# Longer rows for K and V in a cached attention block: 16 KB loads, P transposed on VectorE, PV in four row tiles

## The chip, the cores and the metric

The kernel runs on one core of a Trainium2 chip. The metric is the device time of one execution in microseconds. The time before is the median of three runs.

## The reference

A block of grouped-query attention reads a cache: 32 batches, 4 new tokens each, 32 query heads, 4 heads of K and V, 2048 cached tokens of 128 elements, all in bf16.

```python
q = (x @ wq).reshape(B, Sq, Hq, Dh).transpose(0, 2, 1, 3)      # B 32, Sq 4, Hq 32, Dh 128
k = jnp.repeat(k_cache, rep, axis=1)                           # k_cache: [32, 4, 2048, 128]
v = jnp.repeat(v_cache, rep, axis=1)
scores = jnp.einsum("bhqd,bhkd->bhqk", q, k) * (Dh ** -0.5)
p = softmax(scores, axis=-1)
o = jnp.einsum("bhqk,bhkd->bhqd", p, v)
return o.transpose(0, 2, 1, 3).reshape(B, Sq, Hq * Dh) @ wo    # D 1024
```

One batch needs 2 MB of K and 2 MB of V. For each head of K and V there are 32 rows of queries (8 heads of 4 tokens), so the scores of a batch are 128 rows (4 heads by 32) by 2048 tokens.

## The kernel before

A small `Program` class holds a list of operations for each engine, in the order in which that engine runs them, with the events that each waits for. The order is written out by hand, and no planner moves anything.

**Loads.** SP issues everything: x, then a `stream` of 2 MB loads that go round 9 slots: four of wq, K of batches 0 to 2, then V of a batch and K of the batch three further on, in turn, and at the end four of wo (the last one in four parts). A load waits until the load that had its slot before is used up (`freed`). K and V of one batch are laid out as "g (p t) d -> p g (t d)" with p = 128: each partition gets 16 consecutive tokens of each of the four heads, which is four rows of 4 KB. A row of wq is 16 KB, a row of wo 2 KB.

**Start.** x is transposed, the Q projection runs over eight banks of PSUM, and K of the first two batches is transposed.

**One batch i on TensorE:** `qk(i)`, then `pv(i-1)`, then the transposes of K of batch i+2 (`kt_fill`, eight fills of eight 128x128 tiles), then the transposes of P of batch i (`tr_fill`, four fills of four tiles).

- `qk` makes 16 matmuls in four column tiles of 32, one tile for each head, 512 tokens each, into the four banks of `ps_s`.
- The fills go round a ring of four banks of PSUM, a, b, c and o. VectorE copies some of them to SBUF and ScalarE the others (`consumer`): of K's eight fills five go to VectorE, of P's four two.
- P is transposed by matmuls against a diagonal matrix, `diag`, that holds the reciprocal of each row's sum, so that P is normalized in the same step.
- `pv` makes 64 matmuls of a full 128x128 array with 32 columns each, 16 accumulating over the tokens for each of the four heads, into bank o.

**VectorE** takes the maximum of each row over the 2048 scores (line 379), scales it (380), copies the output of the batch before into `oT_sb` (368), makes reciprocal and `diag` (388, 389), and copies its share of the fills (353). **ScalarE** makes exp with the row's sum (408) and copies its share (355). The next `qk` waits for exp of the batch before, as the scores have one set of banks.

**End.** After the last `pv` the output projection, 64 matmuls of 512 columns over the four loads of wo (line 318), two copies, and the store.

Of the kernel before, what the change touches and what calls it, by code (L numbers as in the profile page):

```python
# [6 lines left out]
ALU = mybir.AluOpType  # L7
# [47 lines left out]
def bass_standalone__gqa_block_cached__sampling_kernel(  # L55
# [17 lines left out]
    G = Hkv  # L73
    scale = float(Dh) ** -0.5
    NSLOT = 9
    SLOT = 8192
    NRING = 4
    KT_FILLS = 2 * G
    TR_FILLS = 4
    AHEAD = 2  # L80
    WQ_LOADS = 4
    WO_LOADS = 4
    HPL = Hq // WO_LOADS

# [5 lines left out]
    with ExitStack() as es:  # L90
        sb = lambda name, shape, dt: es.enter_context(nc.sbuf_tensor(name, shape, dt))
        slots = sb("slots", [128, NSLOT, SLOT], BF16)
        KT_sb = sb("KT_sb", [128, 2, G, Sk], BF16)
        QT_sb = sb("QT_sb", [128, B, Hq, Sq], BF16)
        oT_sb = sb("oT_sb", [128, Hq, NT], BF16)
        pp_sb = sb("pp_sb", [128, 2, Sk], BF16)
        ident = sb("ident", [128, 128], BF16)
        diag = sb("diag", [128, 2, 128], BF16)
# [4 lines left out]
        P_sb = pp_sb[:, 0, :]  # L103
        PT_sb = pp_sb[:, 1, :].rearrange("p (t r) -> p t r", r=128)
        x_sb = pp_sb[:, 0, 0:D]
        xT_sb = pp_sb[:, 0, D:2 * D].rearrange("p (a b) -> p a b", b=128)
        out_sb = pp_sb[:, 1, 0:D]

        ps_s = es.enter_context(nc.psum_tensor("ps_s", [128, Sk], F32))
        ring = [es.enter_context(nc.psum_tensor(f"ps_{c}", [128, 512], F32)) for c in "abco"]  # L110
        ring_f32 = [p[:, :] for p in ring]
        ring_bf16 = [p.bitcast(BF16) for p in ring_f32]
        ps_o = ring_f32[3]
# [3 lines left out]
        for n in ["x", "out"] + [f"slot{i}" for i in range(NSLOT)] + [f"wo{i}" for i in range(4)]:  # L117
            pr.sems[n] = es.enter_context(nc.semaphore(f"s_{n}"))
# [3 lines left out]
        for b in range(AHEAD + 1):  # L122
            stream.append(("k", b))
        for b in range(B):
            stream.append(("v", b))
            if b + AHEAD + 1 < B:
                stream.append(("k", b + AHEAD + 1))
# [13 lines left out]
        pr.load("sp", lambda e: e.dma_start(x_sb, x_flat[:, :]), "x", "x", 16)  # L141
        for n, l in enumerate(stream):
            kind, i = l
            waits = [freed(stream[n - NSLOT])] if n >= NSLOT else []
            s, v = f"slot{n % NSLOT}", 16 * (n // NSLOT + 1)
            if kind == "wq":
                fn = lambda e, l=l, i=i: e.dma_start(slot(l), wq_v[:, i, :])  # L147
            elif kind in "kv":
                src = (k_cache if kind == "k" else v_cache)[i].rearrange("g (p t) d -> p g (t d)", p=128)
                fn = lambda e, l=l, src=src: e.dma_start(slot(l).rearrange("p (g f) -> p g f", g=G), src)  # L150
            if kind != "wo":
                pr.load("sp", fn, l, s, v, waits)
                continue
            last = i == WO_LOADS - 1
            parts = 4 if last else 1
            per = HPL // parts
            for q in range(parts):
                fn = lambda e, l=l, i=i, q=q, per=per: e.dma_start(
                    slot(l)[:, q * per * D:(q + 1) * per * D].rearrange("p (h n) -> p h n", n=D),
                    wo_v[:, i * HPL + q * per:i * HPL + (q + 1) * per, :],  # L160
                )
                if last:
                    pr.load("sp", fn, ("wo", i, q), f"wo{q}", 16, waits)
                else:
                    pr.load("sp", fn, l, s, v, waits)
# [4 lines left out]
        jobs = [("kt", b, f) for b in range(AHEAD) for f in range(KT_FILLS)]  # L170
        for i in range(B):
            if i + AHEAD < B:
                jobs += [("kt", i + AHEAD, f) for f in range(KT_FILLS)]
            jobs += [("tr", i, f) for f in range(TR_FILLS)]
        job_index = {j: n for n, j in enumerate(jobs)}

        def consumer(job):
            kind, _, f = job
            if kind == "kt":
                return "act" if f in (4, 6, 7) else "dve"  # L180
            return "dve" if f in (0, 2) else "act"

        def ring_waits(job):
            n = job_index[job]
            if n < NRING:
                return [("q_evac", n)]
            w = [("evac",) + jobs[n - NRING]]
            if n % NRING == 3:
                b = job[1] - AHEAD - 1 if job[0] == "kt" else job[1] - 1
                if b >= 0:  # L190
                    w.append(("ot", b))
            return w


        pr.op("pool", lambda e: e.memset(ident[:], 0.0), [], "zero")
        pr.op("pool", lambda e: e.affine_select(
            out=ident[:], in_=ident[:], compare_op=ALU.not_equal, fill=1.0, base=0,
            pattern=[[-1, 128]], channel_multiplier=1), ["zero"], "ident")
# [33 lines left out]
        def kt_fill(b, f):  # L232
            job = ("kt", b, f)
            dst = ring_bf16[job_index[job] % NRING]
            g, half = f // 2, f % 2

            def fn(e):
                for q in range(8):
                    t = half * 8 + q
                    ins = e.transpose(  # L240
                        dst[:, q * 128:(q + 1) * 128],
                        slot(("k", b))[:, (g * NKT + t) * Dh:(g * NKT + t + 1) * Dh],
                        ident[:, :],
                    )
                return ins

            pr.op("pe", fn, [("k", b)] + ring_waits(job), job)

        def tr_fill(b, f):
            job = ("tr", b, f)  # L250
            dst = ring_f32[job_index[job] % NRING]

            def fn(e):
                for q in range(4):
                    t = f * 4 + q
                    ins = e.matmul(dst[:, q * 128:(q + 1) * 128], lhsT=P_sb[:, t * 128:(t + 1) * 128],  # L256
                                   rhs=diag[:, b % 2, :], start=True, stop=True)
                return ins

            pr.op("pe", fn, [("exp", b), ("diag", b)] + ring_waits(job), job)  # L260

        def pv(b):
            def fn(e):
                v = slot(("v", b))
                for g in range(G):
                    for t in range(NKT):
                        ins = e.matmul(  # L267
                            ps_o[:, 32 * g:32 * (g + 1)],
                            lhsT=v[:, (g * NKT + t) * Dh:(g * NKT + t + 1) * Dh],
                            rhs=PT_sb[:, t, 32 * g:32 * (g + 1)],  # L270
                            start=(t == 0),
                            stop=(t == NKT - 1),
                        )
                return ins

            w = [("v", b)] + [("evac", "tr", b, f) for f in range(TR_FILLS)]
            if b > 0:
                w.append(("ot", b - 1))
            pr.op("pe", fn, w, ("pv", b))

        def qk(i):
            def fn(e):
                for c in range(Sk // 512):
                    for g in range(G):
# [3 lines left out]
                            rhs=KT_sb[:, i % 2, g, c * 512:(c + 1) * 512],  # L288
# [4 lines left out]
                return ins  # L293

            w = [("evac", "kt", i, f) for f in range(KT_FILLS)]
# [175 lines left out]
```

## Time and profile before

| | |
|---|---|
| median of three runs | 389.67 us (389.29 to 390.6) |
| profiled execution | 388.88 us |
| its span, first to last instruction | 386.9 us |
| mean granted TensorE clock | 0.938 of full speed |
| read from HBM | 151.26 MB, 392 GB/s over the span |
| busy: TensorE, VectorE, ScalarE | 296.0, 242.4, 196.6 us |

The profile is of one execution. A page gives busy times, the span in 40 slices (tenths of busy time, granted clock, GB/s), the DMA queues, the chain of work that ended last, and the costliest groups of instructions. In a group's row stand line, engine, operation, output and inputs, shapes and count, then busy time and mean duration in ns of one, then the idle time before them and what ended it. In a row of the timeline stand start and duration in microseconds, engine, line and operation. "PEld" is TensorE's loading of weights. In a row of the stretches stand the stretch, its length, each engine's busy time (with its count of instructions), the granted clock, the share of the DMA engines and GB/s.

### The profile page before, as it was taken

How to read it: one execution, taken by the hardware profiler on the slowest of the kernel's cores; microseconds unless marked ns; L12 is line 12 of the kernel's file. 1: busy time of each engine (PE TensorE's matmuls, PEld its weight loads, DVE VectorE, ACT ScalarE, POOL GpSimd, SP SyncE). 2: the span in 40 equal slices, each digit the busy share in tenths (PEclk: the TensorE clock that was granted, in tenths of full speed). 3: DMA queues.
4: the chain of work that ended last, by engine and by line, in shares of the span. 5: the costliest groups of instructions: out<-in, count | busy, mean ns of one | idle time of the engine just before them, and what ended most of it. 6: DMA issues, size and time to landing. Idle time of an engine off the chain costs nothing.

```text
span 386.9 us, 11667 instructions
## 1 busy us (share of the span) xinstructions
PE 296.0 (77%) x5448; PEld 246.8 (64%) x5448; DVE 242.4 (63%) x390; ACT 196.6 (51%) x230; POOL 0.7 (0%) x6
## 2 busy tenths in 40 slices
PE   2877787776977977878788869877777787886596
PEld 1777576665766766767667657666666677664542
DVE  0026787775777777758777757877777577774400
ACT  1024766652655565466564635666555564664300
POOL 0000000000000000000000000000000000000000
PEclk9999999998999899889898979999999898997689
DMA  8999999999999999999999999999999999999981
GB/s 327 430 412 410 407 404 407 408 408 409 406 406 409 407 409 410 406 409 407 407 409 409 405 410 410 405 409 408 407 407 407 408 409 407 409 408 359 372 327 56
DMA packets 38912, 152.26 MB, mean 393 GB/s; under 512 B 1232, under 2 KB 1232, under 8 KB 38352
## 3 DMA queue, kind: packets, MB, share of 16 engines
q1 hardware_dynamic: 38864, 151.52, 98.5%
q8 instruction: 42, 0.69, 0.7%
q14 instruction: 6, 0.05, 0.0%
HBM read 151.26 MB, written 0.26 MB: 392 GB/s over the span
## 4 chain that ended last, share of the span: by engine, by line
DMA 87%; PE 7%; ACT 2%; DVE 2%; SPq 1%; issue 0%
DMA slots<-in_k_cache_dram 87%; PE ps_s L318 4%; DVE mx L379 1%; ACT pp_sb L408 1%; PE ps_s L285 1%; ACT KT_sb L355 1%; PE ps_a L240 1%; PE ps_o L267 0%; SPq L147 0%; PE ps_o L256 0%; PE ps_a L256 0%; PE ps_b L240 0%; SPq L150 0%; PE ps_c L256 0%; PE ps_b L256 0%
## 5 line engine op out<-in xcount | busy, mean ns | idle before, releaser
L408 ACT ACTIVATE pp_sb<-ps_s,negmx 128x2048 bf16<-128x2048 f32 x32 | 62.9, 1967 | 93.1 <-DVE negmx L380 93.1
L379 DVE TENSOR_REDUCE mx<-ps_s 128x1 f32<-128x2048 f32 x32 | 73.3, 2292 | 35.3 <-PE ps_s L285 35.3
L240 PE MATMUL ps_a<-ident,slots 128*128 128x128 bf16 x512 | 43.8, 234 | 42.2 <-DMA slots<-in_k_cache_dram 41.3
L240 PEld LDWEIGHTS ps_a<-ident,slots 128*128 128x128 bf16 x512 | 33.7, 105 | 46.1 <-DMA slots<-in_k_cache_dram 44.9
L267 PEld LDWEIGHTS ps_o<-pp_sb,slots 128*128 128x128 bf16 x2048 | 53.5, 96 | 14.6 <-issue 13.7
L267 PE MATMUL ps_o<-pp_sb,slots 128*128 128x32 bf16 x2048 | 56.7, 177 | 0.8 <-ACT pp_sb L355 0.8
L355 ACT ACTIVATE KT_sb<-ps_a 128x1024 bf16<-128x1024 bf16 x32 | 32.6, 1020 | 45.6 <-PE ps_a L240 45.6
L240 PE MATMUL ps_o<-ident,slots 128*128 128x128 bf16 x512 | 42.7, 231 | 7.8 <-DVE KT_sb L353 7.8
L353 DVE COPY KT_sb<-ps_b 128x1024 bf16<-128x1024 bf16 x64 | 43.7, 683 | 5.2 <-PE ps_b L240 5.2
L353 DVE COPY KT_sb<-ps_a 128x1024 bf16<-128x1024 bf16 x32 | 22.1, 689 | 35.0 <-PE ps_a L240 35.0
L240 PE MATMUL ps_c<-ident,slots 128*128 128x128 bf16 x512 | 43.3, 233 | 0.7 <-issue 0.7
L240 PE MATMUL ps_b<-ident,slots 128*128 128x128 bf16 x512 | 43.5, 234 | 0.0
L240 PEld LDWEIGHTS ps_o<-ident,slots 128*128 128x128 bf16 x512 | 33.8, 105 | 11.4 <-DVE KT_sb L353 11.2
L240 PEld LDWEIGHTS ps_c<-ident,slots 128*128 128x128 bf16 x512 | 34.8, 105 | 1.5 <-issue 0.9
L240 PEld LDWEIGHTS ps_b<-ident,slots 128*128 128x128 bf16 x512 | 35.2, 106 | 0.4
L285 PE MATMUL ps_s<-KT_sb,QT_sb 128*32 128x512 bf16 x512 | 34.3, 389 | 0.0
L355 ACT ACTIVATE KT_sb<-ps_c 128x1024 bf16<-128x1024 bf16 x32 | 32.7, 1021 | 1.9 <-PE ps_c L240 1.9
L355 ACT ACTIVATE KT_sb<-ps_o 128x1024 bf16<-128x1024 bf16 x32 | 32.9, 1027 | 0.0
L353 DVE CAST pp_sb<-ps_a 128x512 bf16<-128x512 f32 x32 | 22.1, 692 | 12.8 <-PE ps_a L256 12.8
L256 PE MATMUL ps_o<-diag,pp_sb 128*128 128x128 bf16 x128 | 13.2, 227 | 14.7 <-ACT KT_sb L355 14.7
L353 DVE CAST pp_sb<-ps_c 128x512 bf16<-128x512 f32 x32 | 21.9, 685 | 1.9 <-PE ps_c L256 1.6
L353 DVE COPY KT_sb<-ps_c 128x1024 bf16<-128x1024 bf16 x32 | 21.9, 684 | 1.0 <-PE ps_c L240 1.0
(46 smaller groups left out, 244.7 us busy)
## 6 DMA issues: line engine op xcount, KB each, us to landing
slots<-in_k_cache_dram SPq DMA_DIRECT2D x32, 2048.0 KB, 25.0
slots<-in_v_cache_dram SPq DMA_DIRECT2D x32, 2048.0 KB, 24.2
slots<-in_wq_dram SPq DMA_DIRECT2D x4, 2048.0 KB, 14.9
slots<-in_wo_dram SPq DMA_DIRECT2D x3, 2048.0 KB, 25.6
slots<-in_wo_dram SPq DMA_DIRECT2D x4, 512.0 KB, 12.2
pp_sb<-in_x_dram SPq DMA_DIRECT2D x1, 256.0 KB, 2.7
out_dram<-pp_sb SPq DMA_DIRECT2D x1, 256.0 KB, 2.2
```

Of the source, the lines that this page charges most:

```text
L240: ins = e.transpose(dst[:, q * 128:(q + 1) * 128], slot(("k", b))[:, (g * NKT + t) * Dh:(g * NKT + t + 1) * Dh], ident[:, :],)
L256: ins = e.matmul(dst[:, q * 128:(q + 1) * 128], lhsT=P_sb[:, t * 128:(t + 1) * 128], rhs=diag[:, b % 2, :], start=True, stop=True)
L267: ins = e.matmul(ps_o[:, 32 * g:32 * (g + 1)], lhsT=v[:, (g * NKT + t) * Dh:(g * NKT + t + 1) * Dh], rhs=PT_sb[:, t, 32 * g:32 * (g + 1)], ...
L285: ins = e.matmul(ps_s[32 * g:32 * (g + 1), c * 512:(c + 1) * 512], lhsT=QT_sb[:, i, REP * g:REP * (g + 1), :], rhs=KT_sb[:, i % 2, g, c * ...
L318: ins = e.matmul(ps_s[:, c * 512:(c + 1) * 512], lhsT=oT_sb[:, h, :], rhs=w[:, h - i * HPL, c * 512:(c + 1) * 512], start=(h == 0), stop=( ...
L353: pr.op("dve", lambda e: e.tensor_copy(dst, src), w, ("evac",) + job)
L355: pr.op("act", lambda e: e.activation(dst, src, ACT.Copy), w, ("evac",) + job)
L379: pr.op("dve", lambda e, i=i: e.tensor_reduce(mx[:, i:i + 1], ps_s[:, :], AX.X, ALU.max), [("qk", i)], ("max", i))
L408: pr.op("act", lambda e, i=i: e.activation(P_sb, ps_s[:, :], ACT.Exp, bias=negmx[:, i:i + 1], scale=scale, accum_out=ssum[:, i:i + 1]), [( ...
```

## The change

- K and V are laid out as "g (p t) d -> (g p) (t d)" with p = 32: each head has 32 partitions, and each partition 64 consecutive tokens, one row of 16 KB.
- A transpose of K now gives 32 tokens of each of the four heads; `KT_sb` is [d, 64 steps, 4 heads, 32 tokens], and `qk` reads it in runs of 32. `qk` is split in four, each with the wait for its own two fills. VectorE copies fills 0 to 3, ScalarE 4 to 7.
- P is transposed on VectorE in 32x32 blocks, SBUF to SBUF, with one instruction for a batch. `tr_fill` and `diag` go.
- `pv` makes 256 matmuls: 64 steps by four row tiles, one row tile for each head, with 32 tokens of V as the stationary operand and 32 columns. Each head has a bank of the ring to itself. One more matmul writes the reciprocals as a row on all partitions (`R_bank`).
- ScalarE copies that row and the four heads' raw output to SBUF (`raw_evac`), ahead of exp of batch i; VectorE multiplies the two into `oT_sb` (`ot_scale`). The fills of K that follow a `pv` in the ring wait for `raw_evac`, and a `pv` waits for the copies of the last four fills.
- `pv` runs two batches behind `qk` (LAG 2) in place of one; K is loaded four batches ahead of V in place of three; there are 8 slots in place of 9.
- wo is loaded by POOL in 16 parts, each of which waits for V of batch 30 to land, besides its slot.

The core of the diff:

```diff
-    NSLOT = 9
+    NSLOT = 8
+    LAG = 2
+    LEAD = AHEAD + LAG
...
-                src = (k_cache if kind == "k" else v_cache)[i].rearrange("g (p t) d -> p g (t d)", p=128)
+                src = k_cache[i].rearrange("g (p t) d -> (g p) (t d)", p=KP)
+                src = v_cache[i].rearrange("g (p t) d -> (g p) (t d)", p=KP)
...
+                for q in range(WO_PARTS):
+                    part = slot(l)[:, q * WO_PER * D:(q + 1) * WO_PER * D].rearrange("p (h n) -> p h n", n=D)
+                    h0 = i * HPL + q * WO_PER
+                    pr.load("pool", fetch(part, wo_v[:, h0:h0 + WO_PER, :]), ("wo", i, q), f"wo{i * WO_PARTS + q}", 16, waits + [("v", B - 2)])
...
         def pv(b):
+            waits = list(bank_last.values())
+            for n in range(NRING):
+                bank_last[n] = ("raw", b)
             def fn(e):
-                v = slot(("v", b))
-                for g in range(G):
-                    for t in range(NKT):
+                v = slot(("v", b)).rearrange("p (t d) -> p t d", d=Dh)
+                for t in range(KTOK):
+                    for g in range(G):
+                        rows = slice(KP * g, KP * (g + 1))
                         ins = e.matmul(
-                            ps_o[:, 32 * g:32 * (g + 1)],
-                            lhsT=v[:, (g * NKT + t) * Dh:(g * NKT + t + 1) * Dh],
-                            rhs=PT_sb[:, t, 32 * g:32 * (g + 1)],
+                            pv_bank[g],
+                            lhsT=v[rows, t, :],
+                            rhs=PT_buf[rows, b % NPT, t, :],
+                            tile_position=(KP * g, 0),
                         )
+                return e.matmul(R_bank, lhsT=rinv16[:, b:b + 1].to_broadcast([128, 128]), rhs=ident[:, :],
+                                start=True, stop=True)
+            pr.op("pe", fn, [("v", b), ("pt", b), ("rinv16", b)] + waits, ("pv", b))
...
         for i in range(B):
             qk(i)
-            if i >= 1:
-                pv(i - 1)
+            if i >= LAG:
+                pv(i - LAG)
             if i + AHEAD < B:
                 for f in range(KT_FILLS):
                     kt_fill(i + AHEAD, f)
-            for f in range(TR_FILLS):
-                tr_fill(i, f)
...
+        def raw_evac(b):
+            src = ps_r[:, :].rearrange("p (g f) -> p g f", g=G)[:, :, 0:KP]
+            pr.op("act", lambda e: e.activation(R_sb[:, b % 2, :], R_bank, ACT.Copy),
+                  [("pv", b)] + ([("ot", b - 2)] if b >= 2 else []))
+            pr.op("act", lambda e: e.activation(o_sb[:, b % 2, :, :], src, ACT.Copy), [("pv", b)], ("raw", b))
...
+            pr.op("dve", lambda e: e.tensor_tensor(dst, raw, row, op=ALU.mult), [("raw", b)], ("ot", b))
...
+            if i >= LAG:
+                ot_scale(i - LAG)
             pr.op("dve", lambda e, i=i: e.reciprocal(rinv[:, i:i + 1], ssum[:, i:i + 1]), [("exp", i)], ("rinv", i))
+            pr.op("dve", lambda e, i=i: e.tensor_copy(rinv16[:, i:i + 1], rinv[:, i:i + 1]), [("rinv", i)], ("rinv16", i))
+            pr.op("dve", lambda e, i=i: e.transpose(PT_buf[:, i % NPT, :, :].rearrange("p t r -> p (t r)"), P_sb),
+                  [("exp", i)] + ([("pv", i - NPT)] if i >= NPT else []), ("pt", i))
...
         for i in range(B):
+            if i >= LAG:
+                raw_evac(i - LAG)
             pr.op("act", lambda e, i=i: e.activation(
                 P_sb, ps_s[:, :], ACT.Exp, bias=negmx[:, i:i + 1], scale=scale, accum_out=ssum[:, i:i + 1]),
-                [("negmax", i)] + ([("tr", i - 1, TR_FILLS - 1)] if i > 0 else []), ("exp", i))
+                [("negmax", i)] + ([("pt", i - 1)] if i > 0 else []), ("exp", i))
```

More of the change, by code (lines that the diff above doesn't have):

```diff
@@ L195, in bass_standalone__gqa_block_cached__sampling_kernel, with take @@
[L195 to L198, printed above, removed]
+        bank_of = {}
+        bank_last = {n: ("q_evac", n) for n in range(NRING)}
+        turn = [0]
+        def take(job):
+            bank = turn[0] % NRING
+            turn[0] += 1
+            bank_of[job] = bank
+            before = bank_last[bank]
+            bank_last[bank] = ("evac",) + job
+            return bank, [before]
@@ L245, in fn @@
                 return ins
[L247 to L251, printed above, removed]
-            def fn(e):
[L254 to L260, printed above, removed]
@@ L308, in bass_standalone__gqa_block_cached__sampling_kernel, with oproj @@
                     kt_fill(i + AHEAD, f)
[L309 to L313 removed]
+        for b in range(B - LAG, B):
+            pv(b)
+        def oproj(i, h0, n):
             def fn(e):
```

206 lines of the change are left out of this document (80 added, 126 removed).

## The prediction

> **What bounds the kernel now.** I read the page's DMA slices first, then the chain, then the groups by form, then stretches of the timeline. The first question is whether the transfers or an engine set the pace.
>
> ```profile
> PE 296.0 (77%) x5448; PEld 246.8 (64%) x5448; DVE 242.4 (63%) x390; ACT 196.6 (51%) x230; POOL 0.7 (0%) x6
> PEclk9999999998999899889898979999999898997689
> GB/s 327 430 412 410 407 404 407 408 408 409 406 406 409 407 409 410 406 409 407 407 409 409 405 410 410 405 409 408 407 407 407 408 409 407 409 408 359 372 327 56
> DMA packets 38912, 152.26 MB, mean 393 GB/s; under 512 B 1232, under 2 KB 1232, under 8 KB 38352
> q8 instruction: 42, 0.69, 0.7%
> DMA 87%; PE 7%; ACT 2%; DVE 2%; SPq 1%; issue 0%
> slots<-in_k_cache_dram SPq DMA_DIRECT2D x32, 2048.0 KB, 25.0
> ```
>
> 87% of the chain is a K load, and the rate stands at 404 to 412 GB/s in 34 slices: the kernel runs at the pace of its transfers. The one faster slice is the second, at 430. It belongs to the wq loads, and they are the packets that are not "under 8 KB": a wq row is 16 KB of consecutive bytes, a K or V row today is 4 KB. The stretches:
>
> ```profile
> core 0: us, PE busy (x) PEld busy (x) DVE busy (x) ACT busy (x) POOL busy (x), PEclk, DMA share, GB/s
> 8.00:22.00 14.00, 10.87 (x166) 10.70 (x167) 0.00 (x0) 0.00 (x0) 0.00 (x0) 1.00 1.01 431
> 30.00:340.00 310.00, 245.17 (x4724) 208.37 (x4725) 221.76 (x357) 179.79 (x209) 0.00 (x0) 0.94 1.03 408
> 352.00:368.00 16.00, 9.25 (x176) 7.28 (x176) 6.25 (x11) 6.32 (x8) 0.00 (x0) 0.64 0.99 358
> 372.00:379.00 7.00, 7.00 (x34) 3.15 (x33) 0.00 (x0) 0.00 (x0) 0.00 (x0) 1.00 0.64 241
> ```
>
> Both of the first two are full (DMA share about 1): 431 GB/s with 16 KB rows, 408 with 4 KB, and 358 in the tail, where wo's 2 KB rows prevail. Row length alone orders the three. From 372 to 379 the queue runs thin.
>
> ```profile
> 366.10 1.87 PE L267 MATMUL ps_o<-pp_sb,slots 128*128 128x32 bf16 x64 [0.78 <-ACT pp_sb L355]
> 368.45 14.86 PE L318 MATMUL ps_s<-slots,oT_sb 128*128 128x512 bf16 x64 [0.47 <-DVE oT_sb L368]
> 383.34 0.69 DVE L398 CAST pp_sb<-ps_s 128x512 bf16<-128x512 f32 x1 [15.04 <-PE ps_s L318]
> ```
>
> The output projection starts after the last PV and ends at 383.3, 4.3 us after the transfers.
>
> **The change: transfers.** K and V are 64 loads of 2.097 MB, 134.2 MB. At 408 GB/s they take 329.0 us, at 431 they take 311.4: 17.6 us less, and a batch (one K, one V) needs 9.73 us instead of 10.28. That is the gain, if the engines keep that pace. Eight slots for nine leave three to four loads queued ahead, about 15 us: no cost. TensorE's instructions about double (per batch 64+64+64+16 pairs become 64+16+256+1), so some 0.7 MB more comes on the instruction queue: 0.7% of 387 us again, but on a busy engine; I take 1.5 us, between 0 and 2.9.
>
> **The tail.** wo goes from SP's queue to POOL's, in 16 parts behind V30's landing. The trace has no transfer issued by POOL; its rate lies between wo's own 358 and, if issuing held it up, the 241 of the thin stretch (8.39 MB in 23 or 35 us). I take 358, nearest because the rows are the same. SP now has only K and V ahead of its last instruction; POOL has nothing behind its waits. The thin stretch (7 us at 241 where 358 was to be had) is worth 7 x 117/358 = 2.3 us, and goes, since all parts are queued by then. The projection follows the parts: after the last one 4 of its 64 matmuls remain (14.86/64 = 0.23 each, 0.9 us) and 0.3 of signals, so it ends 1.2 instead of 4.3 us after the transfers: -3.1.
>
> **The engines.** These rows price what a batch holds after the change:
>
> ```profile
> L379 DVE TENSOR_REDUCE mx<-ps_s 128x1 f32<-128x2048 f32 x32 | 73.3, 2292 | 35.3 <-PE ps_s L285 35.3
> L408 ACT ACTIVATE pp_sb<-ps_s,negmx 128x2048 bf16<-128x2048 f32 x32 | 62.9, 1967 | 93.1 <-DVE negmx L380 93.1
> L408 ACT ACTIVATION_READ_ACCUMULATOR pp_sb<-ps_s,negmx 128x1 f32 x32 | 6.2, 193 | 0.0
> L355 ACT ACTIVATE pp_sb<-ps_b 128x512 bf16<-128x512 f32 x32 | 19.4, 607 | 3.4 <-PE ps_b L256 3.4
> L368 DVE CAST oT_sb<-ps_o 128x128 bf16<-128x128 f32 x32 | 9.0, 281 | 2.4 <-PE ps_o L267 2.4
> L388 DVE RECIPROCAL rinv<-ssum 128x1 f32<-128x1 f32 x32 | 5.0, 157 | 5.3 <-ACT pp_sb L408 4.2
> L380 DVE TENSOR_SCALAR negmx<-mx 128x1 f32<-128x1 f32 x32 | 4.9, 154 | 1.1
> 191.10 1.02 ACT L355 ACTIVATE KT_sb<-ps_c 128x1024 bf16<-128x1024 bf16 x1
> 192.01 1.03 ACT L355 ACTIVATE KT_sb<-ps_o 128x1024 bf16<-128x1024 bf16 x1
> 190.05 0.68 DVE L353 COPY KT_sb<-ps_o 128x1024 bf16<-128x1024 bf16 x1
> 190.65 0.68 DVE L353 COPY KT_sb<-ps_b 128x1024 bf16<-128x1024 bf16 x1
> 196.49 0.62 PE L240 MATMUL ps_a<-ident,slots 128*128 128x128 bf16 x8 [0.32 <-DMA slots<-in_k_cache_dram]
> 196.94 0.61 PE L240 MATMUL ps_b<-ident,slots 128*128 128x128 bf16 x8
> ```
>
> DVE loses two 512-wide copies, diag and one K copy, and gains the P transpose. No row has a DVE transpose. Its bounds: 1.3 us, two of the 1024-wide copies, and 4.6, twice the reduction over the same 2048 elements. I take the reduction's 2.3, the row of equal length on the same engine. DVE per batch: 2.3 + 0.15 + 4 x 0.6 + 0.3 (scale) + 0.16 + 0.15 (rinv16) + 2.3 = 7.8 us. [...]
>
> ACT: exp and accumulator 2.16; four K copies that start 0.91 apart, 3.75; two copies of 128 columns from PSUM. 1024 to 512 columns goes from 1.02 to 0.61, so 128 give about 0.29 each. 6.5 us in all.
>
> PE: fills 0.45 each, 3.6; QK 1.05. Its strided K reads cost nothing to 1 us (nothing hides them); I take 0. Diagonal matmuls go. PV is the open term:
>
> ```profile
> 193.42 0.12 PEld L285 LDWEIGHTS ps_s<-KT_sb,QT_sb 128*32 128x32 bf16 x8
> 193.42 0.40 PE L285 MATMUL ps_s<-KT_sb,QT_sb 128*32 128x512 bf16 x4
> 194.40 1.77 PE L267 MATMUL ps_o<-pp_sb,slots 128*128 128x32 bf16 x64
> ```
>
> Today's PV: 64 matmuls of 32 columns in 1.77 us, of which the last runs 0.177: one per 25 ns. The two QK rows are those that had begun within 0.04 us (a window from 193.41 to 193.46): four matmuls in four column tiles, and the weights of the next four, side by side. The change has 256 matmuls in four row tiles. Bounds: 256 x 25 ns = 6.4 us if row tiles take turns; 64 x 25 = 1.6 if four run at once. I take 1.6 plus 0.3 for switching modes and the R row: P = 1.9, since QK's tiles are the only tiled matmuls in the trace and run at once.
>
> **The cycle.** The new waits make a loop. PV shares its four banks with the fills, so the fills wait for the two raw copies on ACT; exp stands behind those on ACT; ACT's four K copies stand behind exp; and the next PV waits for the last of them. From the end of one PV: raw copies 0.6, exp and accumulator to 2.75, ACT's first K copy held by its fill to 3.1, four copies to 6.9, signal 0.1, then PV: 7.0 + P = 8.9 us. QK (ends at 5.6) and the fills (4.5) lie beside it. DVE's 7.8 fit too. Against 9.73 of transfers 0.8 us are to spare, so transfers still set the pace, and the engines' price is 0.
>
> **The sum**, against the profiled execution's own 388.88 us (span 386.9 and 2.0 around it): -17.6 rows, -2.3 thin stretch, -3.1 projection, +1.5 instructions = 367.4. The median of the runs shown is 0.8 above that execution, so about 368.
>
> **Rivals.** If the loop binds, the first PV starts at 48.6 as now, 29 cycles follow, then two PVs, 1 us to scale, the projection and what follows it (14.9 + 3.6 + 2.0):
>
> ```profile
> 48.62 0.54 PE L267 MATMUL ps_o<-pp_sb,slots 128*128 128x32 bf16 x15
> ```
>
> T = 48.6 + 29 x (7.0 + P) + 2P + 21.5 = 273 + 31P. It passes 367.4 at P = 3.0 and 388.9 at P = 3.7, 14.6 ns per matmul.
>
> 1. *Slower: row tiles take turns.* P = 6.4 + 0.3, T = 481. For it: 25 ns did not change with anything in PV, 512 instructions per batch must reach TensorE at a pace that no row shows, and 32 columns are small already. Against it: QK's tiles. Chance 0.20, taking in any pace beyond 14.6 ns. [...]
>
> 2. *Weights not hidden inside a row tile.* A tile then alternates 25 ns of weights and 25 of matmul: 64 x 50 = 3.2, P = 3.5, T = 381.5. Against it: the QK rows show eight weight loads begun with four matmuls still running, the second four in the same columns. Chance 0.10. [...]
>
> 3. *Rows do not matter* with every engine writing beside the transfers: -17.6 falls away, 385. For it: the 431 was seen with DVE and ACT idle. Against it: 408 holds level in all other slices, busy or less so. Chance 0.04.
>
> 4. *DVE or the clock binds.* If the transpose takes over 4.2 us, DVE's sum passes 9.73; at 4.6, 10.1 x 32 gives some 13 us more, 380. And at half clock a fill takes twice as long, ACT's copies wait for it and the cycle is nearly 11: 395 if most cycles ran so. The mean now is 0.94. Chance 0.06.
>
> **How the numbers follow.** Forecast 0.60, rivals 0.20, 0.10, 0.04 and 0.06. Faster by over 0.3% (what a measurement of this kernel tells from no change): the forecast, rivals 2 and 3 and half of 4, less a little for their upper ends: 0.75. Same 0.03. Slower 0.22. The forecast's own range is 363 (no instruction cost, projection right behind) to 375 (wo slower on POOL's queue). For 8 in 10 it must take in rivals 2 to 4: 362 to 396.
>
> **What would show it.** Right: K and V stretches at about 430 GB/s, no packets of 4 KB, the chain still on K or V loads, PV of 257 matmuls in about 2 us, the DVE transpose at 2.3 us, PE's waits ended by K loads. Wrong: a PV of 4 us or more, a DMA share well under 1 in mid-run, the chain going round PV, the raw copies, exp and ACT's K copies. A rate that stays at 408 with DMA full would be rival 3; a last wo part landing long after 361 would be POOL's queue.

## The result, and the profile after

The changed kernel takes 577.2 us (median of four runs, 574.72 to 577.9) against 389.55 us for the kernel before beside it: a ratio of 1.480, 95% interval 1.475 to 1.485. The prediction was 368 us, range 362 to 396. It was wrong in sign and in size. From here on, the working of the prediction is compared with the profiled execution of 577.11 us (span 575.2).

The page of the changed kernel: busy times, granted clock, GB/s by slice, packets, the instruction queue, and the chain's shares.

```profile
PE 335.1 (58%) x11110; PEld 286.9 (50%) x11112; DVE 252.6 (44%) x326; ACT 201.5 (35%) x262; POOL 12.3 (2%) x22
PEclk9899567776677777666777776667777676667559
GB/s 363 430 422 433 420 426 424 321 239 227 273 218 245 276 294 293 220 239 269 239 239 271 293 260 223 255 259 214 264 294 295 239 276 243 236 191 291 3 5 18
DMA packets 12476, 152.99 MB, mean 266 GB/s; under 512 B 1376, under 2 KB 1376, under 8 KB 3680
q8 instruction: 87, 1.43, 0.9%
PE 41%; issue 30%; ACT 22%; DMA 5%; DVE 2%; SPq 0%
```

The long rows are there (38352 packets under 8 KB have become 3680), and while the loads can run ahead into free slots they move at 420 to 433 GB/s. Then the rate falls to some 250: the loads now wait for slots (SP stands 252.5 us in all before the end of a PV, 184.9 before fills of K). No engine is busier than 58%. 30% of the chain is "issue", time in which an engine waited for nothing that the profile shows; before it was 0%. On the instruction queue 87 packets carry 1.43 MB, 16 KB each, where 42 carried 0.69 MB. TensorE has 11110 + 11112 = 22222 instructions here and had 10896 before; divided by 256 that is 86.8 and 42.6, so one packet is a block of 256 TensorE instructions.

The waits of the changed kernel (us in total, times, longest):

```profile
ACT R_sb L335 <- PE ps_r L263: 248.6, 32, 12.9
PEld ps_r L255 <- issue: 212.0, 69, 5.2
PE ps_r L255 <- issue: 152.4, 36, 5.1
```

PV (line 255) stands still for 152 us in 36 gaps, a little over one a batch, of up to 5.1 us. The groups:

```profile
L255 PE MATMUL ps_r<-PT_sb,slots 32*128 32x32 bf16 x8192 | 78.3, 181 | 193.8 <-issue 152.4
L373 DVE STREAM_TRANSPOSE PT_sb<-P_sb 128x2048 bf16<-128x2048 bf16 x32 | 73.6, 2301 | 0.0
L272 PE MATMUL ps_s<-KT_sb,QT_sb 128*32 128x512 bf16 x512 | 34.9, 394 | 2.5 <-ACT P_sb L388 2.5
```

PV's own work is 78.3 us for 32 batches, 2.4 us each, but 193.8 us of idle time stand ahead of its matmuls. The DVE transpose takes 2.30 us, and QK with its runs of 32 is as quick as before (394 ns a matmul against 389, 1.05 us for the 16 in both). One cycle, in the timeline (start, duration, engine, line; copies of R at both ends):

```profile
283.36 0.28 ACT L335 ACTIVATE R_sb<-ps_r 128x128 f32<-128x128 f32 x1 [7.39 <-PE ps_r L263]
283.69 1.97 ACT L388 ACTIVATE P_sb<-ps_s,negmx 128x2048 bf16<-128x2048 f32 x1
283.95 5.25 PE L236 MATMUL ps_r<-ident,slots 128*128 128x128 bf16 x64 [0.63 <-ACT o_sb L337]
287.89 3.77 ACT L331 ACTIVATE KT_sb<-ps_r 128x1024 bf16<-128x1024 bf16 x4 [2.15 <-PE ps_r L236]
...
291.81 1.52 PE L255 MATMUL ps_r<-PT_sb,slots 32*128 32x32 bf16 x168 [1.64 <-ACT KT_sb L331]
...
298.47 0.89 PE L255 MATMUL ps_r<-PT_sb,slots 32*128 32x32 bf16 x88 [5.14 <-issue]
299.29 0.11 PEld L263 LDWEIGHTS ps_r<-ident,rinv 128*128 128x128 bf16 x1
...
299.62 0.28 ACT L335 ACTIVATE R_sb<-ps_r 128x128 f32<-128x128 f32 x1 [7.95 <-PE ps_r L263]
```

The cycle is 299.62 - 283.36 = 16.26 us. PV runs 168 of its matmuls in 1.52 us, stops for 5.14, and runs the other 88 in 0.89. Stretches, first the two that were shown of before, then that gap cut in pieces:

```profile
core 0: us, PE busy (x) PEld busy (x) DVE busy (x) ACT busy (x) POOL busy (x), PEclk, DMA share, GB/s
8.00:22.00 14.00, 13.23 (x190) 13.12 (x191) 0.00 (x0) 0.00 (x0) 0.00 (x0) 1.00 1.01 430
30.00:340.00 310.00, 181.25 (x6025) 158.12 (x6025) 151.15 (x197) 122.21 (x155) 0.00 (x0) 0.72 0.77 297
...
293.30:296.10 2.80, 0.03 (x4) 0.00 (x0) 0.00 (x0) 0.00 (x0) 0.00 (x0) 0.62 0.88 375
296.10:297.10 1.00, 0.00 (x0) 0.00 (x0) 0.00 (x0) 0.00 (x0) 0.00 (x0) 0.50 0.08 25
297.10:298.40 1.30, 0.00 (x0) 0.00 (x0) 0.00 (x0) 0.00 (x0) 0.00 (x0) 0.50 0.00 0
```

For 2.8 us a K load is still landing and everything else is idle. Then 25 GB/s flow for 1.0 us, 25 KB, of which 16 are one packet of the instruction queue; 1.3 us later PV goes on. In the gap the granted clock falls to 0.50, and it stays there into the fills of K behind a gap: those of the cycle above take 5.25 us for their 64 transposes, at 0.50 from 284 to 287 us and 0.69 on average (3.6 was forecast, from a full clock).

### The profile page after: what moved, and what is told of

Same layout as the page of the kernel before. It is cut to its first block, busy times and chain, and to the rows that moved or that the text cites. A ratio compares the mean times of both kernels' runs of the same rounds, so it can differ in the third digit from the quotient of the medians.

```text
span 575.2 us, 22999 instructions
## 1 busy us (share of the span) xinstructions
PE 335.1 (58%) x11110; PEld 286.9 (50%) x11112; DVE 252.6 (44%) x326; ACT 201.5 (35%) x262; POOL 12.3 (2%) x22
## 2 busy tenths in 40 slices
DMA packets 12476, 152.99 MB, mean 266 GB/s; under 512 B 1376, under 2 KB 1376, under 8 KB 3680
## 3 DMA queue, kind: packets, MB, share of 16 engines
q8 instruction: 87, 1.43, 0.9%
## 4 chain that ended last, share of the span: by engine, by line
PE 41%; issue 30%; ACT 22%; DMA 5%; DVE 2%; SPq 0%
PE ps_r L236 22%; ACT KT_sb L331 18%; PE ps_r L255 14%; DMA slots<-in_k_cache_dram 5%; PE ps_s L305 3%; ACT R_sb L335 1%; PE ps_r L263 1%; ACT o_sb L337 1%; DVE mx L362 1%; PE ps_s L272 1%; ACT P_sb L388 1%; DVE KT_sb L329 0%; DVE PT_sb L373 0%; SPq L159 0%; DVE PT_sb L377 0%
## 5 line engine op out<-in xcount | busy, mean ns | idle before, releaser
L236 PE MATMUL ps_r<-ident,slots 128*128 128x128 bf16 x2048 | 181.9, 273 | 24.1 <-ACT o_sb L337 17.5
L329 DVE COPY KT_sb<-ps_r 128x1024 bf16<-128x1024 bf16 x128 | 87.1, 690 | 245.6 <-PE ps_r L236 245.4
L255 PE MATMUL ps_r<-PT_sb,slots 32*128 32x32 bf16 x8192 | 78.3, 181 | 193.8 <-issue 152.4
L236 PEld LDWEIGHTS ps_r<-ident,slots 128*128 128x128 bf16 x2048 | 174.8, 128 | 31.9 <-issue 25.6
L255 PEld LDWEIGHTS ps_r<-PT_sb,slots 32*128 32x128 bf16 x8192 | 72.1, 94 | 212.2 <-issue 212.0
L331 ACT ACTIVATE KT_sb<-ps_r 128x1024 bf16<-128x1024 bf16 x128 | 120.7, 1030 | 76.4 <-PE ps_r L236 76.4
L373 DVE STREAM_TRANSPOSE PT_sb<-P_sb 128x2048 bf16<-128x2048 bf16 x32 | 73.6, 2301 | 0.0
L388 ACT ACTIVATE P_sb<-ps_s,negmx 128x2048 bf16<-128x2048 f32 x32 | 63.1, 1971 | 2.6 <-DVE negmx L363 2.6
L159 POOL DMA_DIRECT2D slots<-in_wo_dram x16 | 11.6, 730 | 511.5 <-PE ps_r L263 504.9
L305 PE MATMUL ps_s<-slots,oT_sb 128*128 128x512 bf16 x62 | 15.6, 417 | 1.4 <-DVE oT_sb L351 1.3
```

Of the source, the lines that this page charges most:

```text
L236: ins = e.transpose(dst[:, q * 128:(q + 1) * 128], slot(("k", b))[:, t * Dh:(t + 1) * Dh], ident[:, :],)
L255: ins = e.matmul(pv_bank[g], lhsT=v[rows, t, :], rhs=PT_buf[rows, b % NPT, t, :], start=(t == 0), stop=(t == KTOK - 1), tile_position=(KP ...
L305: ins = e.matmul(ps_s[:, c * 512:(c + 1) * 512], lhsT=oT_sb[:, h, :], rhs=w[:, h - i * HPL, c * 512:(c + 1) * 512], start=(h == 0), stop=( ...
L329: pr.op("dve", lambda e: e.tensor_copy(dst, src), w, ("evac",) + job)
L331: pr.op("act", lambda e: e.activation(dst, src, ACT.Copy), w, ("evac",) + job)
L373: pr.op("dve", lambda e, i=i: e.transpose(PT_buf[:, i % NPT, :, :].rearrange("p t r -> p (t r)"), P_sb), [("exp", i)] + ([("pv", i - NPT)] ...
```

## The experiments

**Theory A:** TensorE runs out of instructions. A batch has 674 of them (before: 320), and 512 belong to PV, which uses them up in some 2 us; TensorE then stands still for 5 us until the next block of 256 is there. **Rivals:** B, row tiles or their loop are slow in themselves; C, the 16 KB packets hold up the instruction block, and shorter ones would not; D, any data transfer holds it up.

Counted in the trace of the changed kernel, with TensorE's semaphore instructions among the others, PV has 35 gaps of over 1.5 us, of 4.94 us in the middle case. All of them fall at the same instruction count modulo 256, and in each of them a block's transfer ends. That made A the first theory; the runs had to show that it is the cause.

### Fewer PV matmuls: a quarter and a half

Both leave out part of PV's tokens (every fourth, or every second of the 64 steps is done) and keep everything else: loads, row tiles, waits, copies.

```diff
-                for t in range(KTOK):
+                for t in range(0, KTOK, 4):        # the other run: 2
```

> The changed kernel with every fourth step of PV alone (64 matmuls in place of 256; three quarters of the sum over tokens are left out). Theory A, TensorE runs out of instructions: in the changed kernel's trace the 5 us gaps inside PV stand where a multiple of 256 instructions is used up, and a transfer of one block of instructions lies inside each. With 290 instructions a batch in place of 674 a block lasts some 9 us: no gap of over 3 us inside PV, the clock back above 0.9, transfers set the pace, 365 to 390 us. Theory B, the loop through PV, raw copies, exp and ACT's copies is itself that long, at the lower clock: only three quarters of PV's 2.1 us of work go, 16.4 - 1.6 us a batch, 577 - 50 = 527 us.

> The changed kernel with every second step of PV (128 matmuls; half of the sum is left out). A: a burst of 258 instructions crosses one block's end in place of two, the next end follows soon in some batches only, so a gap of 2 to 4 us in a part of the batches: 395 to 460 us. B: half of PV's 2.1 us goes, 577 - 34 = 543 us.

A quarter: 371.95 us, ratio 0.955 (0.951 to 0.959). A half: 432.58 us, ratio 1.111 (1.105 to 1.117). The page of the quarter run, then its stretch and its end in the timeline:

```profile
GB/s 330 432 425 424 434 427 425 421 421 424 427 425 431 425 425 427 429 424 422 427 429 426 425 424 424 424 425 424 427 429 424 425 429 429 421 424 291 374 387 178
q8 instruction: 39, 0.64, 0.7%
DMA 80%; PE 10%; DVE 3%; POOL 3%; ACT 3%; SPq 1%; issue 1%; POOLq 0%
```

```profile
30.00:340.00 310.00, 215.35 (x4569) 180.76 (x4566) 240.92 (x313) 196.78 (x250) 0.46 (x1) 0.85 1.00 423
```

```profile
364.30 1.04 PE L305 MATMUL ps_s<-slots,oT_sb 128*128 128x512 bf16 x4 [0.30 <-DMA slots<-in_wo_dram]
365.56 1.04 PE L305 MATMUL ps_s<-slots,oT_sb 128*128 128x512 bf16 x4 [0.22 <-DMA slots<-in_wo_dram]
```

With 290 instructions a batch the transfers set the pace again, and the output projection follows the parts of wo. The granted clock is 0.85 in mid-run; the "above 0.9" expected with theory A did not come. The half run's waits:

```profile
PEld ps_r L236 <- issue: 46.2, 41, 4.5
PE ps_r L255 <- issue: 39.9, 14, 5.9
PE ps_r L236 <- issue: 21.5, 11, 4.4
```

At 418 a batch some of the batches stop, now also in the fills behind PV. From 290 to 418 to 674 instructions the time goes 372, 433, 577: A was right twice, B (527 and 543) wrong twice. 514 instructions in a row ran dry, 130 did not.

The packets of the instruction queue, set beside the instruction count, show more. In the kernel before, TensorE crosses a boundary of 256 instructions 42 times, and each crossing is followed by one packet, 1.3 to 4.2 us later; in the changed kernel there are 87 of each. Where TensorE ran dry, it went on 1.4 us after the end of the packet that followed the crossing before: one block was ordered ahead, and no second one lay ready. So a block has a price from crossing to crossing. In the changed kernel it is 6.0 us in the middle case (1.1 of work, 4.9 of gap) and 5.7 to 7.8 in 30 of the 35, and the kernel before never crosses twice within less than 6.1 us.

### Four pieces of 4 KB in each row, and wider PV matmuls

```diff
-                pr.load("sp", fetch(slot(l), src), l, s, v, waits)
+                for q in range(4):
+                    cols = slice(q * 2048, (q + 1) * 2048)
+                    count[s] += 16
+                    pr.load("sp", fetch(slot(l)[:, cols], src[:, cols]), l if q == 3 else (l, q), s, count[s], waits)
```

> The changed kernel, K and V loaded as four transfers of 4 KB per partition in place of one of 16 KB; layout and result as in the changed kernel. Theory C, a block of instructions waits behind the 16 KB packets (0.6 us each) on its DMA engine: packets of a quarter shorten the 2.8 us between the start of a gap and the start of the block's transfer to about 1, the gap from 5.1 to some 3.3, and the time from 577 to about 520. A without C (the wait is the supply's own): gaps stay within 0.3 us of 5.1 and the time within 8 us of 577, as transfers are not the bound. B: 577.

586.0 us, ratio 1.508 (1.500 to 1.516). Its waits:

```profile
PE ps_r L258 <- issue: 158.4, 41, 6.4
```

At the boundaries of 256 instructions there are 35 gaps again, of 4.99 us in the middle case (4.94 with 16 KB packets). C fell, though a packet of 16 KB takes 0.61 us in the middle case of the changed kernel's trace, close to the 0.6 that C took. The time is 9 us above 577, where 8 at most was expected; with the shorter packets the loads move at 406 to 413 GB/s before the gaps set in, where the changed kernel's moved at 420 to 433. The other run makes each PV matmul 128 columns wide (its extra columns are not used), with the same number of instructions:

```diff
-                            pv_bank[g],
+                            ring_f32[g][:, 0:4 * KP],
-                            rhs=PT_buf[rows, b % NPT, t, :],
+                            rhs=PT_buf[rows, b % NPT, min(t, KTOK - 4):min(t, KTOK - 4) + 4, :],
```

> The changed kernel with 128 columns in place of 32 in each of PV's 256 matmuls (same number of instructions, four times the columns; what is added is not used, and the last three steps read neighbouring blocks of P). A: the longer work, 64 x 53 ns = 3.4 us in place of 2.1, lies in the time in which the next block is on its way: time within 15 us of 577. B: PV is 1.3 us longer in each batch, 577 + 42 = 619 us.

592.1 us, ratio 1.519 (1.513 to 1.525), at the edge of A's range and far from B's 619. TensorE is busy for 54 us more (389.0 against 335.1), the time grows by 15, and the gaps shrink:

```profile
PE ps_r L255 <- issue: 113.0, 34, 4.5
```

Work put into PV comes mostly out of the gaps, as A has it: while TensorE works longer on a block, the next one is on its way. From crossing to crossing it is 5.8 us (1.8 of work, 3.9 of gap in the middle case). The 54 us are net of the fills of K, which are busy for 16 us less (165.8 against 181.9) with the granted clock at 0.82 in mid-run in place of 0.72.

### An eighth of the traffic

From the 17th load of the stream on, each K and V load brings one eighth of its columns; PV and QK then work on what the slots held before.

```diff
+                cols = slice(0, SLOT if n < 16 else 1024)
+                pr.load("sp", fetch(slot(l)[:, cols], src[:, cols]), l, s, v, waits)
```

> The changed kernel, where from the 17th load on K and V bring an eighth of each row (2 KB of 16; the rest of a slot keeps old data). Theory D, the blocks of instructions are late because the data transfers hold their queue or the memory: with an eighth of the traffic the wait inside a gap falls from 2.6 us to under 1, the gap from 4.9 to about 3, the time to 500 or less. A without D (the supply has this delay by itself): gap within 0.5 us of 4.9, time within 15 us of 577.

511.7 us, ratio 1.313 (1.303 to 1.323). Its page and its waits:

```profile
GB/s 353 431 426 425 431 426 259 25 45 44 28 39 45 44 44 39 29 45 44 45 44 41 27 44 45 43 35 35 44 45 44 45 43 25 322 201 144 4 4 21
```

```profile
PE ps_r L253 <- issue: 88.2, 36, 5.0
```

The time is above the 500 that D allowed, and far below 577. Measured in the trace, the gaps at the boundaries (35 and 36 of them) went from 4.94 us to 2.48 in the middle case. In the changed kernel the block's transfer starts 2.62 us after TensorE has run dry, takes 0.95, and TensorE goes on 1.40 after its end. Here it starts as TensorE runs dry (0.13 us before that), takes 1.09, and TensorE goes on 1.42 after it. So the data in flight cost about 2.5 us of each gap (4.94 - 2.48), with packets of 16 KB as with 4 KB (4.99); what is left is 3.6 us from crossing to crossing. The changed kernel itself agrees: its four such gaps after the last load has landed are 1.7 to 2.7 us. Even at 25 to 45 GB/s of data the supply is too slow for this PV. How the data transfers hold the block back stays open.

### The kernel before with 704 instructions a batch

Each PV matmul is split in four of 8 columns. No row tiles, no 16 KB rows, nothing else of the change:

```diff
+                        for q in range(4):
+                                ps_o[:, 32 * g + 8 * q:32 * g + 8 * (q + 1)],
+                                lhsT=v[:, (g * NKT + t) * Dh:(g * NKT + t + 1) * Dh],
+                                rhs=PT_sb[:, t, 32 * g + 8 * q:32 * g + 8 * (q + 1)],
```

> The kernel before (4 KB rows, full array, no row tiles), each PV matmul of 32 columns split into four of 8: 256 matmuls, the same sum, 704 instructions a batch in place of 320. At 25 ns each PV takes 6.4 us in place of 1.6, and TensorE has 12 us of work a batch. A: a block of 256 instructions lasts 3.2 us inside PV, less than it takes to bring one, so gaps of 1.5 to 3 us inside PV at multiples of 256 instructions, 16 to 18 us a batch, 520 to 590 us. Rival, the gaps belong to row tiles or to 16 KB rows: no gaps, some 13 us a batch, 440 to 460 us.

601.5 us, ratio 1.543 (1.532 to 1.555), just above A's range. Its waits, then one PV of it in the timeline:

```profile
PE ps_o L268 <- issue: 59.6, 33, 3.2
```

```profile
312.32 4.88 PE L268 MATMUL ps_o<-pp_sb,slots 128*128 128x8 bf16 x189
318.98 1.18 PE L268 MATMUL ps_o<-pp_sb,slots 128*128 128x8 bf16 x38 [1.78 <-issue]
```

The same gaps, at the same boundary, appear in a kernel without any of the change's other parts. They are shorter, since full-array matmuls take 26 ns each (4.88/189), so that 128 of them with their weight loads, one block, last 3.3 us. From crossing to crossing it is 5.7 us (3.2 of work, 2.5 of gap in the middle case), close to the changed kernel's 6.0. Much of this kernel's time is TensorE's own: 493 us busy, 82%, at a clock of 0.78. So it shows that instructions alone bring the gaps, not that the gaps alone make the 212 us by which it is slower than the kernel before.

### One part at a time: wo on POOL, then K in long rows

The kernel before with wo in 16 parts on POOL and nothing else:

> The kernel before with the change's tail alone: wo by POOL in 16 parts behind V30. By the prediction's terms -2.3 (thin stretch) and -3.1 (projection behind the parts): 389.5 - 5.4 = 384. If POOL's queue is slower than SP's: 389 or more.

388.8 against 389.1 us, ratio 0.999 (0.997 to 1.002): no change. Its timeline:

```profile
368.36 15.37 PE L313 MATMUL ps_s<-slots,oT_sb 128*128 128x512 bf16 x62 [0.86 <-DVE oT_sb L360]
```

The projection starts where it did (368.45 before), behind the last PV, and not behind the wo parts. The last two batches' chain of maximum, exp, transposes and PV sets the end there.

The rest asks what 16 KB rows bring in a complete computation with 320 instructions a batch. All versions give K 16 KB rows and leave V in 4 KB rows and P on TensorE; all but the second have wo on POOL. K's tokens then come out of the transposes in another order than V's partitions have them, and each version puts the reordering in another place:

```diff
+                    src = k_cache[i].rearrange("g (p t) d -> (g p) (t d)", p=32)
 # 1: QK reads K with elements 4 KB apart
+                            rhs=KT_sb[:, i % 2, :, g, :].rearrange("d (j u) p -> d u p j", u=16)[:, 4 * c:4 * c + 4, :, :],
 # 2: V in four DMAs of 32 partitions (wo stays on SP); QK reads runs of 32
+                            slot(l)[32 * j:32 * (j + 1), :].rearrange("p (g f) -> p g f", g=G), src[j])
 # 3: exp writes with elements 8 bytes apart
+                P_sb.rearrange("r (u p j) -> r j u p", u=16, j=4), ps_s[:, :].rearrange("r (j u p) -> r j u p", j=4, u=16), ACT.Exp,
 # 4: V in four DMAs of 128 partitions whose source starts with a dimension of 4
+                    src = v_cache[i].rearrange("g (p j u) d -> g j p (u d)", p=32, j=4)
 # 5: the copies from PSUM read with elements 256 bytes apart
+                src = ring_bf16[n % NRING].rearrange("p (u j m) -> p u m j", u=2, j=4)
```

Place 1:

> The kernel before with K alone in 16 KB rows (the new K layout; V keeps 4 KB rows, P's transposes and PV stay as before, QK reads K in a permuted order so that the tokens match V's), and wo by POOL in 16 parts. 320 instructions a batch as before, so no gaps. Half of the 17.6 us of longer rows and the tail: 389.5 - 8.8 - 5.4 = 375. If QK's strided reads of K take twice as long they add 1 us a batch to TensorE, still hidden: 375. If longer rows gain nothing while the engines work: 384.

426.4 us, ratio 1.094 (1.087 to 1.100). Its timeline:

```profile
210.04 3.62 PE L283 MATMUL ps_s<-KT_sb,QT_sb 128*32 128x512 bf16 x16
```

QK takes 3.62 us instead of 1.05; the maximum waits 114.1 us in all for it (35.3 before), and exp 174.7 for the maximum (93.1 before).

Place 2:

> The kernel before with K alone in 16 KB rows and the rest of it, wo by SP too, as before. So that QK reads K in runs of 32 as in the changed kernel (1.05 us there, 3.6 us with single elements 4 KB apart in the run before), V's rows of 4 KB go to partitions in the order that fits, as four transfers of 32 partitions for each batch. 320 instructions a batch: no gaps inside PV. Half of the bytes at some 425 GB/s (the rate with every fourth step of PV) in place of 408: 67.1 MB take 158 in place of 164.5 us, 389 - 6.5 = 382, between 380 and 384. If the four transfers of 32 partitions are slower than one of 128: 389 or more.

652 us in the median, the runs spread from 616 to 689. The page of the longest:

```profile
GB/s 374 429 269 259 260 256 243 245 245 237 238 227 210 210 203 200 214 240 207 202 207 211 193 193 211 213 155 205 212 215 175 189 195 207 216 160 131 201 270 133
```

With V's loads confined to 32 partitions each, the rate falls to 131 to 270 GB/s from the third slice on, with the DMA engines busy for 0.99 of the stretch from 30 to 340 us, and TensorE waits for the loads (252.5 us in all for K's). Four transfers in place of one are not the cause by themselves: four pieces for a load over all partitions moved at 406 to 413 GB/s above. Why those of 32 partitions are slow stays open.

Place 3:

> The kernel before with K alone in 16 KB rows (V stays in 4 KB rows over all 128 partitions, P is transposed by TensorE, PV is 64 matmuls of the full array, 320 TensorE instructions a batch; wo on POOL, which by itself changed nothing). A transpose of K gives 32 tokens of each head, QK reads it in runs of 32 (1.05 us in the trace of the changed kernel), and exp writes its output permuted, 8 bytes apart, so that the rest is as before. Theory A (rows of 16 KB pay, and only the supply of TensorE's instructions took the gain away): half of the loads at 431 instead of 408 GB/s, 67.1 MB x (1/408 - 1/431) = 8.8 us less, 378 to 384, mid-run at 418 to 421 GB/s, no stretch in which TensorE waits for instructions. Rival (the gain needs both K and V in long rows, or mixed rows run at the slower rate): 387 to 391. If exp's permuted write is slow (over 3.5 us instead of 2.16), the loop max, exp, P's transposes binds as in the run with elements 4 KB apart: over 395.

466.3 us, ratio 1.199 (1.195 to 1.203). Its groups:

```profile
L402 ACT ACTIVATE pp_sb<-ps_s,negmx 128x2048 bf16<-128x2048 f32 x32 | 154.0, 4813 | 112.4 <-DVE negmx L374 112.4
```

exp takes 4.81 us instead of 1.97, behind the maximum as before.

Place 4:

> The kernel before with K alone in 16 KB rows and nothing strided: a transpose of K gives 32 tokens of each head, QK reads the copied K in runs of 32 tokens and in the order that the P transposes want, so exp and the copies write plainly; to match, V goes to the partitions in another order (four DMAs of 512 KB a batch, one for each head, all 128 partitions, rows of 4 KB). 320 TensorE instructions a batch, wo on POOL. Theory A (16 KB rows pay, and in the changed kernel only the supply of TensorE's instructions took the gain away): half of the loads at 431 instead of 408 GB/s, 67.1 MB x (1/408 - 1/431) = 8.8 us less: 378 to 384, mid-run at 417 to 421 GB/s (415 to 419 was seen in the run with K's elements 4 KB apart), exp at 2.16 us again, no stretches in which TensorE waits for instructions. Rival 1 (rows of 16 KB pay only where K and V both have them): 387 to 391, mid-run 408. Rival 2 (the four V DMAs, with neighbouring partitions' rows 32 KB apart in the cache, are slow as those of 32 partitions were): over 395, mid-run under 400 GB/s.

980.6 us, ratio 2.520 (2.508 to 2.532). A stretch in which V alone lands:

```profile
318.00:321.00 3.00, 0.00 (x0) 0.00 (x0) 0.00 (x0) 0.00 (x0) 0.00 (x0) 0.50 0.26 108
```

The DMA share is 0.26 at 108 GB/s, about a quarter of the sixteen engines' time (the view does not tell the engines apart). Rival 2, loads as slow as those of 32 partitions, has the time (over 395) but does not fit this: the slow transfers of place 2 kept the engines busy for 0.99. Why these leave three quarters of the engines' time unused stays open.

Place 5, with five of K's eight fills on VectorE as before, and with four:

> The kernel before with K alone in 16 KB rows, V as before (one DMA, 128 partitions, 4 KB rows), 320 TensorE instructions a batch, wo on POOL. A fill now takes the eight transposes of K that hold 2 x 4 neighbouring tokens, and the copy from PSUM to SBUF reads its source permuted (four elements 256 B apart in PSUM) and writes plainly, so QK, exp and the P transposes are as before. Theory A (16 KB rows pay, and only the supply of TensorE's instructions took the gain of the changed kernel away): 378 to 384 us, mid-run 415 to 421 GB/s, if the permuted copies stay under 0.95 us on VectorE (0.68 before) and 1.6 on ScalarE (1.02). Rival 1 (rows of 16 KB pay only for K and V together): 387 to 391 with the copies as cheap. Rival 2 (the permuted reads cost what exp's permuted write cost, 2.4 times): VectorE 7.6 + 5 x 0.95 = 12.3 us a batch, 400 or more.

> The run with permuted copies from PSUM, with one more of K's eight fills copied by ScalarE (four and four instead of five by VectorE). If the permuted copy is dearer on VectorE alone (1.1 us: 7.6 - 0.7 + 4 x 0.4 = 8.5 us a batch, ScalarE 7.1) this is the faster of the two, 378 to 384 us by theory A against 385 to 395; if it costs nothing on either, both are within 1% of each other; if it is dear on ScalarE (2.45 us: 13 us a batch), this is the slower, over 410.

413.6 us, ratio 1.064 (1.061 to 1.067), and 386.1 us, ratio 0.993 (0.990 to 0.995). The groups of the second one, its chain, its stretch, and its timeline:

```profile
L348 DVE COPY KT_sb<-ps_b 128x1024 bf16<-128x1024 bf16 x64 | 77.9, 1217 | 0.0
L350 ACT ACTIVATE KT_sb<-ps_o 128x1024 bf16<-128x1024 bf16 x64 | 65.0, 1016 | 3.2 <-PE ps_o L239 3.2
```

```profile
DVE 51%; PE 23%; ACT 16%; DMA 7%; issue 2%; SPq 1%
```

```profile
30.00:340.00 310.00, 243.75 (x4811) 194.90 (x4808) 267.02 (x330) 208.91 (x241) 0.00 (x0) 1.00 1.02 416
```

```profile
365.85 15.29 PE L317 MATMUL ps_s<-slots,oT_sb 128*128 128x512 bf16 x64 [0.47 <-DVE oT_sb L363]
```

The permuted copy takes 1.22 us on VectorE (0.68 plain) and no more than a plain one on ScalarE (1.02). The loads move at 416 GB/s in mid-run against 408, with the DMA engines full (1.02). So rows of 16 KB for one tensor alone pay in the rate, and rival 1 fell. The time stayed above the 378 to 384 expected, because the transfers no longer set the pace: only 7% of the chain is DMA, where it was 87%. The loop through VectorE's maximum and dearer copies and ScalarE's copies does, at 10.21 us from one maximum to the next in nearly every batch, where a batch's 4.19 MB need 10.08 at 416 GB/s. The projection starts 2.6 us earlier than before (365.85 against 368.45). This version takes 0.7% less than the kernel before (0.5 to 1.0%).

## Why the prediction was wrong, point by point

- **Instructions: the step that failed.** "TensorE's instructions about double ... I take 1.5 us, between 0 and 2.9." The amount was right (0.74 MB more), though the pairs of before are 64+64+16+16 = 160 a batch, not 64+64+64+16: P's four fills of four tiles are 16. It was priced as traffic on the DMA engines, and its price lies on TensorE: 152 us of standing still in PV, and a clock of 0.50 into the fills behind it. With it fell "the engines' price is 0". At 320 instructions a batch the supply cost nothing that the chain shows ("issue" 0%, no two crossings within less than 6.1 us); at 674 it brought gaps of up to 5.1 us, where 256 instructions were used up in less than about 6 us beside full transfers.
- **The cycle.** The loop was found as it is (PV, raw copies, exp, ACT's K copies, PV), and its order stands in the timeline. Forecast 7.0 + 1.9 = 8.9 us. Measured 8.45 from the raw copies to PV (1.4 more, with the fills at a clock of 0.69), and 7.81 from PV's start to the next raw copies, of which 5.14 are the gap. The 16.26 us are 6.5 over the transfers' 9.73; 30 cycles make 196 of the 209 us by which the forecast was missed.
- **PV itself.** P = 1.9 was nearly right: the 168 and the 88 matmuls together take 2.4 us as the rows count them, with the gap left out. Row tiles run at once: one matmul per 8 to 9 ns, where the full array of before takes 25. The 0.3 us in P were an estimate: R's matmul takes 0.29 us, and no run shows a cost of switching modes by itself. Rival 1 (481) and rival 2 (381.5) name the wrong mechanism, though rival 1's evidence, "512 instructions per batch must reach TensorE at a pace that no row shows", was the right question. I gave it a pace per matmul where it needed a price per block.
- **Transfers.** The rows pay, less than said: 423 GB/s beside busy engines in the quarter run, not 431; the run with four pieces in each row, back at 406 to 413, points to the length of the packets. 134.2 MB at 423 instead of 408 is 317.3 instead of 329.0 us, -11.7 where -17.6 stood. 408 and 423 for one tensor each make 415 together; 416 was measured. Rival 3 fell.
- **The tail.** -2.3 and -3.1 show up where the batches' chain is short: in the quarter run the projection follows the parts, and its 371.78 us are 17.1 below the 388.88. Less 11.7 for the rows, 5.4 remain, which fits the two terms but is a remainder and not measured by itself. Alone on the kernel before they are worth nothing, as a chain that I had not followed to its end took their place.
- **DVE.** 2.3 us for the transpose was forecast, 2.30 measured; rival 4's transpose over 4.2 us did not occur (its price, "some 13 us", is 12 by its own figures). Its half clock did, for a part of the cycle, behind the gap (0.50 from 284 to 287 us).
- **What would show it.** The signs listed for "wrong" came: DMA share 0.77 in mid-run, the chain round PV and ACT's K copies. PV's 4 us came as a gap, not as slow matmuls.

## What to carry to other kernels

Count the instructions that TensorE uses up in a few microseconds, not only their work: 512 in 2 us ran dry where 130 did not, a block of 256 cost about 6 us here beside full transfers, and the waits named "issue" in a matmul group together with the packets of the instruction queue are where it shows. More, smaller instructions that "run at once" can cost more than they save: here PV stood still for 152 us, against the 11.7 us that the rows were worth. And a layout that lengthens transfers has to put its reordering somewhere: here it cost 2.6 us in QK, 2.8 us in exp, three quarters of the DMA engines' time in a load (share 0.26), 0.5 us a copy on VectorE and nothing on ScalarE; price each place before choosing one.

## What the runs showed of the hardware that was not expected

- From one boundary of 256 TensorE instructions to the next, where it ran dry, it took 6.0, 5.8 and 5.7 us beside full transfers in three kernels with different work between (1.1, 1.8 and 3.2 us), and 3.6 with an eighth of the traffic; in the gap shown the granted clock was down to 0.50 before TensorE went on.
- Four row tiles of 32 rows, with 32 moving columns, take a weight load and a matmul each 8 to 9 ns (1.52 us for 168, the last one's own 0.18 included).
- A moving operand with elements 4 KB apart makes QK's 16 matmuls in four column tiles 3.4 times slower (3.62 against 1.05 us); runs of 32 elements cost nothing (1.05 us in both kernels).
- exp from PSUM with its output 8 bytes apart in SBUF took 4.81 instead of 1.97 us, while ScalarE's copy with a source 256 bytes apart in PSUM stayed at 1.02.
